# Turning back riding outputs by a DMA transposition, and placing one PSUM eviction behind another copy, in a two-layer memory transformer on one core

## The chip, the core and the metric

The kernel runs on one core of one Trainium2 chip. The metric is the device time of one execution in microseconds (us). The kernel before took 1631.83 us, the median of three runs (1628.36, 1632.63 and 1631.83). A further execution was profiled; all views below are of that one.

The engines go by the profile's names: PE (matmuls) with PEld (its weight loads), DVE (vector), ACT (scalar), POOL (GpSimd) and SP, which here issues nearly all the DMAs. L497 is line 497 of the kernel before.

## The reference, cut to what matters

Two layers of attention with a carried memory, each followed by a dense ReLU block; both layers use the same weights. x is 2048 tokens by 512, in 64 segments of 32 tokens. There are 32 heads of 128; the memory is 8 tokens.

```python
for s in range(n_seg):                       # strictly in order: mem is carried
    h = concat([mem, xs])                    # 8 + 32 tokens
    q, k, v = h @ Wq, h @ Wk, h @ Wv         # 512 -> 32 x 128
    p = softmax(where(mask, q @ k.T * scale, -1e9))
    o = (p @ v) @ Wo                         # 32 x 128 -> 512
    mem = o[:, :8]; outs.append(o[:, 8:])

x = x + A(layernorm(x)); x = x + B(layernorm(x))   # layer 0
x = x + A(layernorm(x)); x = x + B(layernorm(x))   # layer 1
# B: relu(x @ w1) @ w2, 512 -> 1376 -> 512
```

## The kernel before, in words

**Steps.** The recurrence over segments is the spine. Step k (k = 0 to 67) works on segment k of layer 0 and, four segments behind, on segment k-4 of layer 1, side by side. The order of PE, DVE, ACT and SP is written out by hand (`manual_schedule`): each of them executes its instructions in the order of the code of `step`. POOL's order is the scheduler's.

**One step on PE.** First the q and k products of heads 0 to 15 (`qk`, L601, three batches, evicted at L605 and L607); then the products of the memory tokens with Wv (`memory_values`, L348); in even steps also the values of layer 1 (`values1`); then scores (L641). Then the q and k products of heads 16 to 31, the transposition of the first half's probabilities (`transpose_p`, L680, copied out by DVE and ACT at L681), the second scores, and P times V of the first half (`weighted_v`, L695). Next come fillers, which have their operands ready and cover the softmax of the second half: values for later steps (`v1`, `v0`), dense products (L530, L548), output products (L468, L471). Then the second half's `transpose_p`, more fillers, its P times V, the output product of the memory tokens (`output_mem`, L648), its copy wm_sb (L959), and four small matmuls that turn it (mt, L981). Its copies HT (L984, DVE) and HTm (L986, ACT) open the next step.

**Values go through DRAM.** `group_values` (L341 to L354) makes a [128, 512] product with four column tiles, copies it from PSUM to the tile VmS on ACT (L353), and stores it to DRAM from SP (L354); `load` (L383) brings it back into Vs in the layout that L695 wants. VmS has three buffers. In a step that makes both `v1` and `v0`, four VmS follow one another, so the fourth waits until the first has been stored. The products of `v1` and the second of `v0` take their PSUM tiles from the pool `fill`, which has two buffers and also serves the dense products and the last P times V tile (L688).

**Riders.** The tile HTm holds the memory tokens of a step in 16 columns; the other 16 columns of the 32-wide matmul would be empty. They carry 16 tokens of a layer 0 segment, whose values so come for nothing. In the same way OTm, the operand of `output_mem`, carries 16 tokens of layer 1 outputs of every other block of 64 tokens. Such outputs leave mt with the model dimension on the partitions. ACT copies them into rT (L991), 16 columns in each of four steps. When a block's four pieces are there, in every fourth step (k = 8, 12, ... 64), `riders_back` (L489) turns them back with four matmuls by the identity into a PSUM tile rp of the pool `fill` (L497; L499 for the block of the last time, k = 64), and `riders_add` (L502, L506) adds rp on DVE to the block's residual R. Both stand behind the first q and k products of the step, ahead of `memory_values`.

**Token pairs.** The tile xe (one buffer) holds 128 tokens of x, loaded by `load_pair` in steps with k % 4 = 1, and read last by `pair_normalize` on DVE (L248) at the first q and k batch of a step with k % 4 = 0. Its normalised copy is transposed by a DMA from SP (`transpose_dma`, L264), as are the dense blocks.

Of the kernel before, what the change touches and what calls it, by code (L numbers as in the profile page):

```python
# [7 lines left out]
BF = mybir.dt.bfloat16  # L8
F32 = mybir.dt.float32
# [13 lines left out]
def kernel(  # L23
# [14 lines left out]
    nc = tc.nc  # L38
# [8 lines left out]
    NC4 = Dm // 128  # L47
# [9 lines left out]
    const = ctx.enter_context(tc.tile_pool(name="const", bufs=1))  # L57
    wk = ctx.enter_context(tc.tile_pool(name="wk", bufs=2))
    dram = ctx.enter_context(tc.tile_pool(name="vdram", bufs=2, space=DRAM))
    ps_c = ctx.enter_context(tc.tile_pool(name="ps_c", bufs=3, space=PSUM))  # L60
    ps_s = ctx.enter_context(tc.tile_pool(name="ps_s", bufs=1, space=PSUM))
    ps_wo = ctx.enter_context(tc.tile_pool(name="ps_wo", bufs=1, space=PSUM))
    ps_fill = ctx.enter_context(tc.tile_pool(name="ps_fill", bufs=2, space=PSUM))
# [8 lines left out]
    def rides(b):  # L72

        return b % 2 == 0 and 0 <= b <= RIDE_LAST

    def place(b):

        if rides(b):
            return b + 4, 0 if b == RIDE_LAST else 64
        return b + 2, 64  # L80
# [97 lines left out]
    ident = const.tile([128, 128], BF)  # L178
# [20 lines left out]
    mhalf_t = const.tile([128, 1], F32)  # L199
    nc.vector.memset(mhalf_t[:], -0.5)  # L200

    HTs, HTms = [], []
    for i in range(2):
        t = const.tile([128, NC4, 2, L], BF, name=f"HT{i}")
        nc.vector.memset(t[:], 0.0)
        HTs.append(t)
        t = const.tile([128, NC4, 32], BF, name=f"HTm{i}")
        nc.vector.memset(t[:], 0.0)
        HTms.append(t)
    Vs = const.tile([128, H * Dh], BF)  # L210
    PL = 64 + L
    Pf = const.tile([128, 7 * PL + 128], BF)
# [4 lines left out]
    OTx1 = const.tile([128, H // 2, 128], BF)  # L217
    OTm = const.tile([128, H, 32], BF)
    nc.gpsimd.memset(OTm[:], 0.0)
    rT = const.tile([128, 1 + NC4, 64], BF)  # L220
    nc.gpsimd.memset(rT[:, 0, :], 0.0)
    hT = const.tile([128, NFC, 128], BF)
    nc.gpsimd.memset(hT[F_LAST:128, NFC - 1, :], 0.0)

# [1 line left out]
    for a in range(2):  # L226
        t = ps_s.tile([128, 512], F32, name=f"sp{a}")
# [5 lines left out]
    vmds, vds = {}, {}  # L233
# [45 lines left out]
    def tokens_T(s, lo, n):  # L279

        c = SEG * (s % 4) + lo
        return pairs["T", s // 4][:, :, c:c + n]

    spare = {}
# [51 lines left out]

    vps = {}

    def group_values(lhsT, ii, dst, pool, tag, q, lo=0, hi=NC4, spare=False):  # L341
        if lo == 0:
            vps[tag] = pool.tile([128, 512], F32, tag=tag, name="vp")
        vp = vps[tag]
        for c4 in range(lo, hi):
            for j in range(4):
                n = 4 * ii + j
                nc.tensor.matmul(vp[32 * j:32 * j + 32, :], lhsT=lhsT(c4), rhs=Wv_sb[:, c4, n * 512:(n + 1) * 512],  # L348
                                 start=(c4 == 0), stop=(c4 == NC4 - 1), tile_position=(0, 32 * j))
        if hi < NC4:  # L350
            return
        VmS = wk.tile([128, 512], BF, tag="dnT" if spare else "VmS", bufs=1 if spare else 3, name="VmS")
        nc.scalar.copy(out=VmS[:], in_=vp[:])  # L353
        q.dma_start(out=dst[ii].rearrange("j t e -> (j t) e"), in_=VmS[:])  # L354

    def dram_values(name, tag, bufs):
        return dram.tile([2, 4, 32, 512], BF, tag=tag, bufs=bufs, name=name)
# [2 lines left out]

        return s >= 4 and s % 2 == 0

    def values0(s, ii, q=None, lo=0, hi=NC4):

        if ii == 0 and lo == 0:
            vds[0, s] = dram_values("vd0", "vd0", 4)
        t = tokens_T(s, 0, SEG)
        group_values(lambda c4: t[:, c4, :], ii, vds[0, s], *((ps_fill, "fill") if ii else (ps_c, "c")), q or nc.sync, lo, hi)

    def values1(k, ii, spare=False):  # L370

# [115 lines left out]
    rps = {}  # L487

    def riders_back(b):  # L489

        i, r = place(b)
        rp = rps[b] = ps_fill.tile([128, Dm], F32, tag="fill", name="rp")
        flat = rT[:].rearrange("p c t -> p (c t)")
        for c4 in range(NC4):
            cols = slice(c4 * 128, (c4 + 1) * 128)
            if r:
                nc.tensor.matmul(rp[:, cols], lhsT=flat[:, 64 * c4:64 * c4 + 128], rhs=ident[:], start=True, stop=True)  # L497
            else:
                nc.tensor.matmul(rp[0:64, cols], lhsT=rT[:, 1 + c4, :], rhs=ident[:], start=True, stop=True,  # L499
                                 tile_position=(0, 0))  # L500

    def riders_add(b):  # L502

        (i, r), rp = place(b), rps[b]
        R = R_tiles[i]
        nc.vector.tensor_tensor(out=R[r:r + 64, :], in0=R[r:r + 64, :], in1=rp[r:r + 64, :], op=ALU.add)  # L506
# [167 lines left out]
    def transpose_p():  # L674

        for p, copy in ((0, nc.vector.tensor_copy), (1, nc.scalar.copy)):
            tp = ps_c.tile([128, 4, 2, L], F32, tag="c")
            for sl in range(4):
                c = PL * (4 * p + sl)
                nc.tensor.matmul(tp[:, sl], lhsT=Pf[:, c:c + 128], rhs=ident_q, start=True, stop=True)  # L680
            copy(out=PT[:, 4 * p:4 * p + 4], in_=tp[:])  # L681
# [38 lines left out]
    def outputs_x(k, hf, pvs, q, copy, layers=(0, 1)):  # L720
        for a in layers:
            if (q, a) in pvs:
                h0, n = 16 * hf + 8 * q, L - ahead(k, a)
                c = 64 * a + SEG * (k % 2)
                ot = OTx1 if hf else OTx0[:, k // 2 % 2]
                copy(out=ot[:, 8 * q:8 * q + 8, c:c + n], in_=pvs[q, a][:, :, L - n:L])  # L726
# [7 lines left out]
    def step(k):  # L734
        act = [a for a in range(2) if 0 <= k - a * DELTA < NSEG]
        even = k % 2 == 0
        p = k // 2
# [10 lines left out]
        ride = ride_of(k)  # L748
        back = k // 2 - 4 if k % 4 == 0 and rides(k // 2 - 4) else None
        lone = k == NSTEP - 1  # L750
        HT, HTn = HTs[k % 2], HTs[(k + 1) % 2]
        HTm, HTmn = HTms[k % 2], HTms[(k + 1) % 2]
# [50 lines left out]
        qks = qk(HT, 0, act, after0)  # L803
        if back is not None:
            riders_back(back)
            riders_add(back)
        if dt is not None and not lone and not ahead_T:
            dense_normalize(dt)
        q = nc.sync
# [33 lines left out]
        if not even:  # L843
            i = p + 2 if p % 2 else p + 4
# [22 lines left out]

        def v0(ii):
            if fills_v0(k):
                values0(k + 3, ii)  # L870

        def v1(ii):
            if even and k >= DELTA:
# [26 lines left out]
            outputs_m(k, 0, pvs, 1)  # L900
            outputs_x(k, 0, pvs, 1, nc.scalar.copy)
        v0(0)
        v0(1)
        if k == 2:
            set_products(3, 5)
        hs = (0, 0, 1, 2, 3) if fills_v0(k) else (0, 2, 3, 3, 3)
# [9 lines left out]
        with tc.high_priority(offset=PRIO):  # L916
            for a in act:
                probabilities(1, ess, a, k)
            if first:
                hand_on(dw)  # L920
            transpose_p()
            if k == 0:
                set_evict(3, 0)
                set_products(3, 1)
            if k == 1:
                set_evict(3, 4)
            if k == 2:
                set_evict(3, 5)
                set_products(3, 6)
            if first:  # L930
                block_moments(dw)
# [6 lines left out]
        with tc.high_priority(offset=PRIO):  # L938
            pvs = weighted_v(1, act)
            for q2 in range(2):  # L940
                outputs_m(k, 1, pvs, q2)
            head = act[:1] if nx is not None and nw % 2 == 0 else act
            outputs_x(k, 1, pvs, 0, nc.vector.tensor_copy, head)
            if first:
                block_normalize(dw)
            outputs_x(k, 1, pvs, 1, nc.vector.tensor_copy, head)
            for q2 in range(2):
                outputs_x(k, 1, pvs, q2, nc.vector.tensor_copy, [a for a in act if a not in head])
            if dw is not None and dw >= 3 and not final:
                store(dw)  # L950
            if k == 2:
                set_evict(3, 6)
            if cont:
                output_mem(wo, 0, H - hh)
                if k == 0:
                    set_evict(3, 1)
                    set_values(3, 2, 4)
                output_mem(wo, H - hh, H)
                nc.scalar.copy(out=wm_sb[:], in_=wo[:])  # L959
            if k == 2:  # L960
                set_products(3, 7)
# [12 lines left out]
        s = rider(k + 1)  # L974
        if s is not None:
            nc.gpsimd.tensor_copy(out=HTmn[:, :, 2 * M:32], in_=tokens_T(s, 16 * ((k + 1) % 2), 16))
        if cont:
            with tc.high_priority(offset=PRIO):
                mt = ps_c.tile([128, NC4, 32], F32, tag="c", name="mt")
                for c4 in range(NC4):  # L980
                    nc.tensor.matmul(mt[:, c4, :], lhsT=wm_sb[:, c4 * 128:(c4 + 1) * 128], rhs=sel[:],  # L981
                                     start=True, stop=True)
                lo, hi = cont[0], cont[-1] + 1
                nc.vector.tensor_copy(out=HTn[:, :, lo:hi, 0:M],  # L984
                                      in_=mt[:, :, lo * M:hi * M].rearrange("p c (a m) -> p c a m", m=M))
                nc.scalar.copy(out=HTmn[:, :, lo * M:hi * M], in_=mt[:, :, lo * M:hi * M])  # L986
                if k == 2:
                    set_evict(3, 7)
                if ride is not None:
                    c = 32 * ride[1] + 16 * ride[2]  # L990
                    nc.scalar.copy(out=rT[:, 1:1 + NC4, c:c + 16], in_=mt[:, :, 16:32])  # L991
        if sooner is not None:
            dense_h(sooner, *hs[3:5])
        if w is not None:
# [7 lines left out]
    with tc.manual_schedule(engines={mybir.EngineType.PE, mybir.EngineType.DVE, mybir.EngineType.SP,  # L1002
# [30 lines left out]
        i = NT - 1  # L1033
# [47 lines left out]
```

## Time and profile before

| what | value |
|---|---|
| median of three runs | 1631.83 us |
| the profiled execution: its own time, its span | 1629.76 us, 1628.1 us |
| PE, DVE, ACT, POOL busy | 98%, 66%, 53%, 17% |
| granted PE clock | 1.00 |
| mean DMA rate | 76 GB/s |
| matmuls of `riders_back` (L497, L499) | 56 and 4 |
| `riders_add` (L506) | 15, 692 ns each |
| VmS evictions (L353) | 298, 587 ns each |
| DMA transpositions (L264) | 42 |

The span is the time from the first to the last instruction. PE's busy time is the length of the stretches in which a matmul is under way; matmuls are pipelined, so the duration of one (about 0.2 us for 128 columns) is not what it adds: what it adds is the distance from its start to the next one's start. In the timeline view several instructions of one line are merged into one row, which gives the start of the first, the time to the end of the last, and in brackets how long the engine had stood idle before, and for what.

The steps can be read from the starts of the first L601 group of each: step 12 runs from 300.22 to 323.79 us, step 13 to 348.85, step 14 to 372.69. In the middle of the kernel four steps together take about 94.4 us.

### The profile page before, as it was taken

To read this page: it belongs to the slowest core of one execution; us is meant where nothing else is said; L and a number is where in the kernel's file an instruction comes from. 1 tells how busy PE (TensorE), PEld (TensorE's weight loads), DVE (VectorE), ACT (ScalarE), POOL (GpSimd) and SP (SyncE) were. 2 spreads that over 40 slices of the span, in tenths; PEclk is the share of its full clock that TensorE was granted. 3 is DMA by queue.
4 is the path that set the end of the run, shared out by engine and by line. 5 is a ranking of instruction groups with operands and counts; after the bars stand their busy time and mean duration, and the time that the engine had idled before them with its cause. 6 is when DMAs were issued, how large, how long until landed. Compare 5 with 4: busy or idle time off the path is not lost. (4 is left out here: it accounts for less than half of the span.)

```text
span 1628.1 us, 83294 instructions
## 1 busy us (share of the span) xinstructions
PE 1587.8 (98%) x37231; PEld 1179.9 (72%) x37316; DVE 1079.7 (66%) x2592; ACT 858.3 (53%) x2424; POOL 269.1 (17%) x517
## 2 busy tenths in 40 slices
PE   7899999999999999999999999999999999999998
PEld 4677777777777777777777777777777777777766
DVE  4556766776676677667667766666776666667654
ACT  3455555555555555555555555555555555555543
POOL 1102111111111112111111111111111111111100
PEclk9999999999999999999999999999999999999999
DMA  9832222222222222222222221222222122221111
GB/s 346 258 93 61 72 68 66 69 57 69 56 65 76 71 65 63 64 55 66 74 74 61 66 66 50 71 69 76 60 70 62 56 64 76 66 69 47 54 46 30
DMA packets 132245, 124.14 MB, mean 76 GB/s; under 512 B 36392, under 2 KB 121808, under 8 KB 131152
## 3 DMA queue, kind: packets, MB, share of 16 engines
q1 hardware_dynamic: 129328, 114.62, 24.1%
q8 instruction: 292, 4.78, 1.3%
q0 software_dynamic: 2560, 4.20, 1.2%
q14 instruction: 65, 0.53, 0.1%
HBM read 65.81 MB, written 45.35 MB: 68 GB/s over the span
## 5 line engine op out<-in xcount | busy, mean ns | idle before, releaser
L601 PE MATMUL qp<-HT,Wq_sb 128*128 128x80 bf16 (+1 forms) x8704 | 368.7, 199 | 1.7 <-issue 0.7
L601 PE MATMUL qp<-HT,Wk_sb 128*128 128x80 bf16 (+1 forms) x8704 | 367.7, 199 | 0.6 <-ACT QT L605 0.3
L601 PEld LDWEIGHTS <-Wq_sb 128*128 128x128 bf16 x8704 | 328.3, 99 | 20.3 <-issue 11.9
L601 PEld LDWEIGHTS <-Wk_sb 128*128 128x128 bf16 x8704 | 329.7, 99 | 2.8 <-issue 0.4
L607 DVE CAST KT<-qp 128x480 bf16<-128x480 f32 (+3 forms) x340 | 199.4, 586 | 178.5 <-PE qp L601 172.5
L605 ACT CAST QT<-qp 128x480 bf16<-128x480 f32 (+3 forms) x340 | 172.0, 506 | 207.7 <-PE qp L601 205.3
L353 ACT CAST VmS<-vp 128x512 bf16<-128x512 f32 x298 | 172.0, 587 | 129.2 <-PE vp L348 122.9
L671 POOL TENSOR_TENSOR Pf<-es,sm 128x320 bf16<-128x320 f32 x187 | 135.0, 722 | 590.8 <-ACT QT L605 181.5
L656 DVE TENSOR_REDUCE mx<-sp 128x8 f32<-128x320 f32 x256 | 114.5, 486 | 110.2 <-PE sp L641 109.8
L661 ACT ACTIVATE es<-es 128x320 f32<-128x320 f32 x256 | 110.9, 469 | 77.5 <-DVE es L659 71.2
L668 DVE TENSOR_REDUCE sm<-es 128x8 f32<-128x320 f32 x256 | 120.5, 471 | 24.0 <-ACT es L661 13.6
L348 PE MATMUL vp<-Wv_sb,HTm 128*32 128x512 bf16 x2144 | 128.2, 380 | 2.0 <-issue 1.4
L648 PE MATMUL sp<-Wo_sb,OTm 128*32 128x512 bf16 x2144 | 128.2, 380 | 0.3 <-DMA Wo_sb<-in_A_Wo_dram 0.3
L348 PE MATMUL vp<-Wv_sb,HT 128*32 128x512 bf16 x2048 | 122.6, 380 | 0.0
L468 PE MATMUL wox<-Wo_sb,OTx 128*128 128x512 bf16 x434 | 112.4, 379 | 7.3 <-issue 4.8
L659 DVE TENSOR_TENSOR es<-sp,mx 128x320 f32<-128x320 f32 x256 | 113.3, 481 | 1.1
L726 DVE CAST OTx<-pv 128x256 bf16<-128x256 f32 (+1 forms) x256 | 85.7, 385 | 39.1 <-ACT OTm L718 39.0
L243 POOL TENSOR_TENSOR rstd<-rstd,mhalf_t 128x1 f32<-128x1 f32 x85 | 46.9, 552 | 391.0 <-DVE rstd L242 390.9
L718 ACT CAST OTm<-pv 128x64 bf16<-128x64 f32 (+1 forms) x512 | 93.4, 253 | 31.2 <-PE pv L695 31.2
L681 ACT CAST PT<-tp 128x320 bf16<-128x320 f32 x136 | 58.3, 429 | 67.5 <-PE tp L680 67.2
L726 ACT CAST OTx<-pv 128x256 bf16<-128x256 f32 (+1 forms) x256 | 78.7, 363 | 28.0 <-PE pv L695 28.0
L681 DVE CAST PT<-tp 128x320 bf16<-128x320 f32 x136 | 66.8, 491 | 39.5 <-PE tp L680 38.5
(122 smaller groups left out, 1928.1 us busy)
## 6 DMA issues: line engine op xcount, KB each, us to landing
vd<-VmS SPq DMA_DIRECT2D x164, 128.0 KB
Vs<-vd SPq DMA_DIRECT2D x164, 128.0 KB
vmd<-VmS SPq DMA_DIRECT2D x134, 128.0 KB
Vs<-vmd SPq DMA_DIRECT2D x254, 32.0 KB
Vs<-vmd SPq DMA_DIRECT2D x120, 64.0 KB
Wv_sb<-in_A_Wv_dram SPq DMA_DIRECT2D x4, 1024.0 KB
Wq_sb<-in_A_Wq_dram SPq DMA_DIRECT2D x4, 1024.0 KB
Wk_sb<-in_A_Wk_dram SPq DMA_DIRECT2D x4, 1024.0 KB
```

Of the source, the lines that this page charges most:

```text
L348: nc.tensor.matmul(vp[32 * j:32 * j + 32, :], lhsT=lhsT(c4), rhs=Wv_sb[:, c4, n * 512:(n + 1) * 512], start=(c4 == 0), stop=(c4 == NC4 - 1 ...
L353: nc.scalar.copy(out=VmS[:], in_=vp[:])
L601: nc.tensor.matmul(qp[:, hi, 0:ncol], lhsT=W_sb[:, c4, h * Dh:(h + 1) * Dh], rhs=HT[:, c4, a_lo:a_hi, :], start=(c4 == 0), stop=(c4 == NC4 ...
L605: nc.scalar.copy(out=dst[:, 0:nh, a_lo * L:a_hi * L], in_=qp[:, 0:nh, 0:ncol])
L607: nc.vector.tensor_copy(out=dst[:, 0:nh, a_lo * L:a_hi * L], in_=qp[:, 0:nh, 0:ncol])
L648: nc.tensor.matmul(wo[32 * j:32 * j + 32, :], lhsT=OTm[:, h, :], rhs=Wo_sb[:, h, :], start=(h < 4), stop=(h >= H - 4), tile_position=(0, 3 ...
L656: nc.vector.tensor_reduce(out=mxs[a][:], in_=sp_tiles[a], axis=AX.X, op=ALU.max)
L659: nc.vector.tensor_tensor(out=es[:], in0=sp_tiles[a], in1=mxs[a][:].unsqueeze(2).to_broadcast([128, 8, L]), op=ALU.subtract)
L668: nc.vector.tensor_reduce(out=sm[:], in_=es[:], axis=AX.X, op=ALU.add)
L671: eng.tensor_tensor(out=P[:, :, 64 * a:64 * a + L], in0=es[:], in1=sm[:].unsqueeze(2).to_broadcast([128, 8, L]), op=ALU.mult)
L681: copy(out=PT[:, 4 * p:4 * p + 4], in_=tp[:])
L726: copy(out=ot[:, 8 * q:8 * q + 8, c:c + n], in_=pvs[q, a][:, :, L - n:L])
```

## The change

Three things change.

1. The two HTm tiles become views of one tile rT [128, 4, 128]: columns 0 to 31 and 32 to 63 are the two HTm, columns 64 to 127 the riding outputs (which stood in a tile of their own). All of rT is zeroed at the start by DVE.
2. `riders_back` no longer uses PE, but for the block at k = 64: SP issues one DMA transposition of the whole of rT into a tile rb, which takes the buffer of xe. `riders_add` moves from its place ahead of `memory_values` to the end of the step's output copies (behind the L726 copies of the second half), and reads rb in SBUF and not rp in PSUM.
3. The second eviction of layer 0's values, with its store, is held back where s = k + 3 is above 5: it stands behind `transpose_p` of the second half, so that ACT copies the transposed probabilities (L681) first. In steps 6, 10, ... 50 and 52, 54, ... 60 this applies (17 steps). The unused argument for cutting the value products into ranges is dropped.

```diff
-        HTms.append(t)
+        HTms.append(rT[:, :, 32 * i:32 * i + 32])
...
-    def group_values(lhsT, ii, dst, pool, tag, q, lo=0, hi=NC4, spare=False):
+    def group_values(lhsT, ii, dst, pool, tag, q, spare=False, later=False):
...
+        def evict():
+            VmS = wk.tile([128, 512], BF, tag="dnT" if spare else "VmS", bufs=1 if spare else 3, name="VmS")
+            nc.scalar.copy(out=VmS[:], in_=vp[:])
+            q.dma_start(out=dst[ii].rearrange("j t e -> (j t) e"), in_=VmS[:])
+        if later:
+            return evict
+        evict()
...
     def riders_back(b):
         i, r = place(b)
+        if r:
+            t = wk.tile([128, NC4, 128], BF, tag="xe", bufs=1, name="rb")
+            nc.sync.dma_start_transpose(out=t[:], in_=rT[:].rearrange("p c t -> p (c t)"))
+            rps[b] = t[:].rearrange("p c d -> p (c d)")
+            return
...
-            if r:
-                nc.tensor.matmul(rp[:, cols], lhsT=flat[:, 64 * c4:64 * c4 + 128], rhs=ident[:], start=True, stop=True)
...
         if back is not None:
             riders_back(back)
-            riders_add(back)
+            if place(back)[1] == 0:
+                riders_add(back)
...
-        v0(1)
+        evict_v0 = v0(1)
...
             transpose_p()
+            if evict_v0 is not None:
+                evict_v0()
...
                 outputs_x(k, 1, pvs, q2, nc.vector.tensor_copy, [a for a in act if a not in head])
+            if back is not None and place(back)[1]:
+                riders_add(back)
...
-                    c = 32 * ride[1] + 16 * ride[2]
-                    nc.scalar.copy(out=rT[:, 1:1 + NC4, c:c + 16], in_=mt[:, :, 16:32])
+                    c = 64 + 32 * ride[1] + 16 * ride[2]
+                    nc.scalar.copy(out=rT[:, :, c:c + 16], in_=mt[:, :, 16:32])
```

More of the change, by code (lines that the diff above doesn't have):

```diff
@@ L200 @@
     nc.vector.memset(mhalf_t[:], -0.5)
+    rT = const.tile([128, NC4, 128], BF)
+    nc.vector.memset(rT[:], 0.0)
     HTs, HTms = [], []
@@ L206 @@
         HTs.append(t)
-        t = const.tile([128, NC4, 32], BF, name=f"HTm{i}")
-        nc.vector.memset(t[:], 0.0)
-        HTms.append(t)
+        HTms.append(rT[:, :, 32 * i:32 * i + 32])
     Vs = const.tile([128, H * Dh], BF)
@@ L219 @@
     nc.gpsimd.memset(OTm[:], 0.0)
-    rT = const.tile([128, 1 + NC4, 64], BF)
-    nc.gpsimd.memset(rT[:, 0, :], 0.0)
     hT = const.tile([128, NFC, 128], BF)
@@ L335, in set_store @@
             q.dma_start(out=set_dram[j][:, 512 * lo:512 * hi], in_=src)
-    vps = {}
-    def group_values(lhsT, ii, dst, pool, tag, q, lo=0, hi=NC4, spare=False):
[L342 to L345, printed above, removed]
+    def group_values(lhsT, ii, dst, pool, tag, q, spare=False, later=False):
+        vp = pool.tile([128, 512], F32, tag=tag, name="vp")
+        for c4 in range(NC4):
             for j in range(4):
@@ L349, in group_values @@
                                  start=(c4 == 0), stop=(c4 == NC4 - 1), tile_position=(0, 32 * j))
[L350 to L354, printed above, removed]
+        def evict():
[5 more added lines that the diff above has]
+        evict()
     def dram_values(name, tag, bufs):
@@ L361, in first_rider, with values0 @@
         return s >= 4 and s % 2 == 0
-    def values0(s, ii, q=None, lo=0, hi=NC4):
-        if ii == 0 and lo == 0:
+    def values0(s, ii):
+        if ii == 0:
             vds[0, s] = dram_values("vd0", "vd0", 4)
         t = tokens_T(s, 0, SEG)
-        group_values(lambda c4: t[:, c4, :], ii, vds[0, s], *((ps_fill, "fill") if ii else (ps_c, "c")), q or nc.sync, lo, hi)
+        return group_values(lambda c4: t[:, c4, :], ii, vds[0, s], *((ps_fill, "fill") if ii else (ps_c, "c")), nc.sync,
+                            later=ii == 1 and s > 5)
     def values1(k, ii, spare=False):
@@ L491, in riders_back @@
         i, r = place(b)
+        if r:
[3 more added lines that the diff above has]
+            return
         rp = rps[b] = ps_fill.tile([128, Dm], F32, tag="fill", name="rp")
-        flat = rT[:].rearrange("p c t -> p (c t)")
         for c4 in range(NC4):
-            cols = slice(c4 * 128, (c4 + 1) * 128)
-            if r:
[L497 to L500, printed above, removed]
+            nc.tensor.matmul(rp[0:64, c4 * 128:(c4 + 1) * 128], lhsT=rT[:, c4, 64:128], rhs=ident[:], start=True,
+                             stop=True, tile_position=(0, 0))
     def riders_add(b):
@@ L869, in v0 @@
             if fills_v0(k):
-                values0(k + 3, ii)
+                return values0(k + 3, ii)
         def v1(ii):
```

## The prediction

> **What bounds the kernel.** I read the page first: how busy the engines are, and the clock.
>
> ```profile
> PE 1587.8 (98%) x37231; PEld 1179.9 (72%) x37316; DVE 1079.7 (66%) x2592; ACT 858.3 (53%) x2424; POOL 269.1 (17%) x517
> PEclk9999999999999999999999999999999999999999
> ```
>
> PE is busy for 98% of the span, at full clock: only 40 us in all are without a matmul. So the time is the sum of what PE issues, and a change gains what it takes off PE, or from those 40 us. Who causes them is in the view of waits: on PE itself, most entries are fixed gaps of 0.2 to 0.4 us; one entry bears on the change, PE pv L695 waiting for ACT PT L681, 2.0 us in two waits.
>
> **Part 1, the four matmuls that go.** PE's timeline around `riders_back`, in step 12 (with it) and in step 13 (without):
>
> ```profile
> 304.23 0.74 PE L601 MATMUL qp<-HT,Wk_sb 128*128 128x80 bf16 x16
> 304.81 0.39 PE L497 MATMUL rp<-ident,rT 128*128 128x128 bf16 x4
> 305.12 1.91 PE L348 MATMUL vp<-Wv_sb,HTm 128*32 128x512 bf16 x32
> ```
> ```profile
> 327.80 0.74 PE L601 MATMUL qp<-HT,Wk_sb 128*128 128x80 bf16 x16
> 328.47 0.83 PE L348 MATMUL vp<-Wv_sb,HTm 128*32 128x512 bf16 x12
> ```
>
> One L601 matmul lasts 0.20 us (199 ns, page part 5), so the last of the sixteen starts at 304.23 + 0.74 - 0.20 = 304.77, and L348 follows 0.35 us later. In step 13 the same distance is 328.47 - 328.34 = 0.13 us. So the four matmuls add 0.22 us to PE's order, not the 4 x 0.22 us of their durations. Over the 14 steps (k = 8 to 60): **14 x 0.22 = 3.1 us**. The last block (L499) stays on PE.
>
> Does PE use the 0.22 us? All that PE does next in the step hangs on PE itself: the next wait, for scores (308.69), has its K copy done at 305.50 and its mask at 305.90, and everything behind shifts along. The PSUM buffer that rp no longer takes is asked for by `values1` at 306.86, when its former users, of the step before, are long done. So I count all of it.
>
> **What part 1 adds.** One DMA transposition on SP, each of the 14 times; at step 12 it stands between these two rows:
>
> ```profile
> 300.21 1.94 SPq L383 DMA_DIRECT2D Vs<-vmd  x4
> 306.83 1.20 SPq L354 DMA_DIRECT2D vmd<-VmS  x2
> ```
>
> It waits for rT's last piece (L991, 300.35) and for rb's buffer, which `pair_normalize` reads until 303.12. The same operation on an equal tile (L264) holds SP for 1.2 us: 303.1 to 304.4. Behind it on SP stands the vmd store, which has nothing to store until 306.83. So SP has 2.4 us to spare. The transfer itself is shown at step 13, where such a transposition precedes the store directly:
>
> ```profile
> 328.61 1.20 SPq L264 DMA_TRANSPOSE dnT<-xn  x1
> 330.18 1.69 SPq L354 DMA_DIRECT2D vmd<-VmS  x2
> 332.83 1.33 SPq L383 DMA_DIRECT2D Vs<-vmd  x4
> ```
>
> From the end of the store's issue (331.87) to the load that waits for it: 0.96 us, and 309.84 - 308.03 = 1.81 us in step 12 with no transposition ahead. So a transposition just ahead does not make the store land later. I take 0; the upper bound is in the rivals. The reader of rb, `riders_add`, comes 18 us later.
>
> `riders_add` itself (0.69 us) leaves DVE ahead of the first maximum, where DVE idled 2.48 us (no gain), and goes here:
>
> ```profile
> 320.65 1.15 DVE L726 CAST OTx<-pv 128x256 bf16<-128x256 f32 x4 [0.90 <-ACT OTm L718]
> 323.52 0.22 DVE L984 CAST HT<-mt 128x64 bf16<-128x64 f32 x1 [1.72 <-PE mt L981]
> ```
>
> Behind it is HT, which opens the next step and is on the path; but DVE stood idle 1.72 us for it. 0.69 us fits and leaves 1.0 us. With both operands in SBUF it has no row here; even at twice the time, 1.4 us, it fits: 0. Without that cover it would cost 14 x 0.69 = 10 us. rb holds xe's buffer until 322.5; the next load into xe is issued at 334.20. The shared tile rT makes POOL's and ACT's writes of HTm wait for the transposition, by then 10 us old. The one larger memset at the start (128 x 256 in the changed kernel's list of instructions) stands for three small ones: 0.
>
> [...]
>
> **Part 2, the eviction held back.** Where it matters is step 54, whose ACT rows read:
>
> ```profile
> 1313.84 0.65 ACT L353 CAST VmS<-vp 128x512 bf16<-128x512 f32 x1
> 1316.46 0.58 ACT L353 CAST VmS<-vp 128x512 bf16<-128x512 f32 x1 [1.97 <-DMA vd<-VmS]
> 1316.94 0.43 ACT L681 CAST PT<-tp 128x320 bf16<-128x320 f32 x1
> ...
> 1317.42 0.37 PE L695 MATMUL pv<-PT,Vs 40*128 40x40 bf16 x16 [1.69 <-ACT PT L681]
> ```
>
> The fourth VmS waits for a buffer, that is for a store; the copy PT stands behind it, and PE waits 1.69 us for PT. Held back, PT would be done about 1315.0 (its transposition ran at 1314.08), and this wait goes. What is late next? The second half of L695 writes a tile of the two-buffer pool `fill`, whose turn is the buffer of the very product that the late eviction reads (v1, v1, v0, one dense product, then L695). In the changed kernel's order this shows as a new wait for ACT on that matmul. PE now waits for the eviction's end, 1317.04 instead of PT's end, 1317.37: only **0.33 us** of the 1.69 come back. Step 38 has the same picture (eviction 0.61 us late, PE 0.34 us): 0.3 us. In the common step (step 14), PT today ends just in time; afterwards PT ends some 0.5 us earlier and the eviction where PT ended (367.85 + 0.43 + 0.58 - 0.11 overlap = 368.75, against 368.82): 0, and within 0.1 us either way, that is -0.9 to +0.9 us over the 9 steps of this kind. In six further steps (6, 18, 26, 52, 56, 60) the second half of L695 starts 0.05 to 0.1 us behind the end of the first: 0.3 us together. Where no dense product follows (52, 56, 60) the held-back copy ends some 0.9 us later, at the start of the output copies (L718), whose reader on PE is 0.8 us further on: 0. Sum: **0.33 + 0.3 + 0.3 = about 1.0 us**.
>
> **Sum.** 1629.76 - 3.1 - 1.0 = 1625.7 us against the profiled execution. The median of the runs is 2.1 us above that execution; shifted by the same 4.1 us it gives 1627.7. Both ends are likely; I forecast **1627.0 us**, which is 0.3% below the median. A difference of 0.3% (4.9 us) is about what a measurement of this kernel can tell from none, and the forecast lies on that line.
>
> **Rivals.**
> - *The wait does go.* If the new wait on the `fill` buffer does not bind, the whole of the PT waits comes back: 1.7 + 0.3 and up to 0.9 in small ones. 1629.76 - 3.1 - 2.9 = 1623.8. Against it: the order's new wait. For it: stores are late by chance, and other executions may have more late ones.
> - *The 0.22 us are absorbed.* If a wait later in the step with a fixed time (a DMA's round trip) ends last, part 1 gives nothing: 1629.76 - 1.0 = 1628.8, or 1630.8 from the median. For it: the Vs loads have only some 0.7 us to spare in step 12 (last issue done 312.36; by the store's 1.81 us it lands at 314.2; L695 starts at 314.89). Against it: these loads hang on PE's own products and so shift along.
> - *Slower: the transposition holds up the vmd round trip.* If it ended late enough to delay the vmd store, the Vs loads would land later by as much, and PE would wait for what exceeds 0.7 us. The slowest transposition in the trace (xnT, issued 312.40) still moves a few packets at 316.2, 3.9 us after its issue, where 1.2 to 2.1 us is usual. A store held back by 2 us costs (2 - 0.7) x 14 = 18 us: 1629.76 - 4.1 + 18 = 1644. It decides from an end later than 306.83 + 0.7 = 307.5; the usual end is 305.2, the slowest 307.0. Step 13 speaks against it. [...]
>
> That the change does not do what it says is excluded by its order: PE's differs by just those 56 matmuls, SP's by 14 transpositions.
>
> **Numbers.** The forecast 0.68, the wait goes 0.12, absorbed 0.12, slower 0.08. The forecast's half below the 0.3% line and all of the first rival are "faster": 0.33 + 0.12 = 0.45. The other half and the absorbed case are "same": 0.35 + 0.12 = 0.47. Slower: 0.08. The range takes in the first rival, less the common step's 0.9 us and as much again for what late stores add or spare by chance (1622.0), and the absorbed case from the median with 0.9 us above (1631.7). The slower rival is left out.
>
> **What would show it.** Part 1: no L497, L348 0.13 us behind the last L601 in steps 8, 12, ... 60, those steps 0.22 us shorter (23.57 to 23.35), a transposition on SP at about 3 us into them, DVE still idle ahead of HT. Part 2: PT ahead of the fourth VmS, and PE's waits at L695 named for ACT VmS and not PT, about 0.3 us shorter. I am wrong if PE waits for a DMA at L695, if HT starts later, or if steps other than these change.

## The result and the profile after

The changed kernel takes **1624.24 us**, the median of six runs (1623.53 to 1625.36); the kernel before, beside it, 1630.6 us (six runs, 1628.36 to 1632.63, the three of above among them). The ratio is 0.9958, with a 95% interval of 0.9948 to 0.9968: faster by 0.42%. The forecast was 1627.0, so the gain is larger than forecast. The profiled execution has a time of 1624.61 us and a span of 1622.9 us, 5.15 us less than that of before (1629.76 and 1628.1).

The page of the kernel after, the busy times of the engines:

```profile
PE 1584.0 (98%) x37175; PEld 1176.4 (72%) x37260; DVE 1078.7 (66%) x2591; ACT 859.2 (53%) x2424; POOL 269.9 (17%) x516
```

PE has 56 matmuls fewer and is busy 3.8 us less; its share is the same. Where the 5.15 us come from is read step by step, from the distances between the starts of the first L601 groups: steps 8, 12, ... 60 (those that turn riders back) give -3.8 us, steps 10, 14, ... 58 give -1.1, the first six steps and the two ends -0.3, all others together +0.1. The -0.3 says nothing about the change: in the 14 traces of this document the first six steps take 128.9 to 132.4 us together, with no order by kernel.

**The riders' steps.** An undisturbed one takes 23.22 us where it took 23.57. That is 0.35 us, not the forecast 0.22. PE's timeline of the kernel after at the place of `riders_back`, in step 20 (start, duration, engine, line):

```profile
492.64 0.74 PE L601 MATMUL qp<-HT,Wk_sb 128*128 128x80 bf16 x16
493.31 1.05 PE L343 MATMUL vp<-Wv_sb,rT 128*32 128x512 bf16 x16
```

The last L601 matmul starts at 492.64 + 0.74 - 0.20 = 493.18; the product of the memory tokens (L343, formerly L348) follows 0.13 us later, as in a step without riders. So 0.22 us came off here, as forecast. The other 0.13 us come off later in the step. First DVE, then PE, in step 20 of the kernel before:

```profile
497.93 0.89 DVE L656 TENSOR_REDUCE mx<-sp 128x8 f32<-128x320 f32 x2 [2.48 <-PE sp L641]
498.85 0.89 DVE L659 TENSOR_TENSOR es<-sp,mx 128x320 f32<-128x320 f32 x2
```
```profile
499.75 1.03 PE L601 MATMUL qp<-HT,Wq_sb 128*128 128x80 bf16 x24
500.81 1.02 PE L601 MATMUL qp<-HT,Wk_sb 128*128 128x80 bf16 x24
```

and in the kernel after:

```profile
497.29 0.89 DVE L656 TENSOR_REDUCE mx<-sp 128x8 f32<-128x320 f32 x2 [2.98 <-PE sp L641]
498.09 0.88 DVE L659 TENSOR_TENSOR es<-sp,mx 128x320 f32<-128x320 f32 x2
```
```profile
499.11 1.03 PE L601 MATMUL qp<-HT,Wq_sb 128*128 128x80 bf16 x24
500.03 1.02 PE L601 MATMUL qp<-HT,Wk_sb 128*128 128x80 bf16 x24
```

From the first maximum (L656) to the first subtraction (L659) it was 0.92 us and is 0.80: before, L659 started 0.03 us behind the end of the second maximum; now it starts 0.08 us ahead of that end, as it did and does in all steps without riders. This holds in all 14 riders' steps. A step without riders in the kernel before, step 11:

```profile
285.25 0.89 DVE L656 TENSOR_REDUCE mx<-sp 128x8 f32<-128x320 f32 x2 [1.26 <-PE sp L641]
286.06 0.88 DVE L659 TENSOR_TENSOR es<-sp,mx 128x320 f32<-128x320 f32 x2
```

The exponentials and the QT copies on ACT follow as much earlier, and a QT copy frees the PSUM buffer of the next K batch: from the Wq group to the Wk group PE took 1.06 us and takes 0.92. So `riders_add`, which stood ahead of the maxima, had been costing 0.13 us a step, though DVE idled 2.48 us behind it. Why, is the subject of experiments 2 to 4.

**What part 1 added.** SP in step 20 of the kernel after:

```profile
491.63 1.24 SPq L494 DMA_TRANSPOSE rb<-rT  x1
495.02 1.20 SPq L349 DMA_DIRECT2D vmd<-VmS  x2
```

The transposition stands 3.0 us into the step and holds SP until 492.87; the vmd store comes 2.15 us later, when its data are there. DVE at the end of the step:

```profile
508.70 1.15 DVE L726 CAST OTx<-pv 128x256 bf16<-128x256 f32 x4 [0.90 <-ACT OTm L718]
509.88 0.69 DVE L506 TENSOR_TENSOR R<-R,rb 64x512 f32<-64x512 f32 x1
511.56 0.23 DVE L989 CAST HT<-mt 128x64 bf16<-128x64 f32 x1 [0.99 <-PE mt L986]
```

`riders_add` takes 0.69 us also with both operands in SBUF and leaves DVE idle for 0.99 us ahead of HT (forecast 1.0). One thing the prediction had otherwise: the transposition is not 10 us old when POOL writes the shared tile rT. In all 14 cases POOL's next copy into rT (L981) waits for it, until 5.4 to 7.4 us into the step (step 60: 3.6). Nothing on the path follows from this: PE's one wait for a POOL copy into this tile, 0.6 us, was there before (0.7 us, HTm).

**Part 2.** PE's longest waits at L695 are named for the eviction and no longer for ACT's copy PT. From the views of waits before and after (us in total, times, longest):

```profile
PE pv L695 <- ACT PT L681: 2.0, 2, 1.7
```
```profile
PE pv L695 <- ACT VmS L348: 1.0, 2, 0.7
```

A late store now shows like this, ACT and then PE in step 50:

```profile
1215.28 0.43 ACT L681 CAST PT<-tp 128x320 bf16<-128x320 f32 x1
1216.46 0.59 ACT L348 CAST VmS<-vp 128x512 bf16<-128x512 f32 x1 [0.75 <-DMA vd<-VmS]
```
```profile
1216.02 0.39 PE L695 MATMUL pv<-PT,Vs 40*128 40x40 bf16 x17
1217.10 0.35 PE L695 MATMUL pv<-PT,Vs 40*128 40x40 bf16 x15 [0.69 <-ACT VmS L348]
```

PT is done in time and the first half of L695 runs; the second half waits for the eviction, whose PSUM buffer it takes. The steps that run longer are 26, 38 and 54 before (0.2, 0.5 and 1.85 us longer than their like) and 18, 30 and 50 after (0.5, 0.2 and 0.85). Undisturbed steps of this kind take 23.86 us in both.

The steps are not drawn afresh in each execution. In the six traces of kernels that turn the riders back on PE, step 38 is over 0.1 us longer in all six and step 54 in five; in the eight traces of kernels with the transposition, neither is in any, but 18 and 50 are in seven each. So the -1.1 us of the profiled pair is not part 2 alone, but also a shift of the steps that have late stores.

What holding back is worth in one late step can be read from the start of the late eviction. At its old place, a step in which it waits for a store is longer than 23.86 us by as much as it starts later than 19.08 us into the step (step 54 before: 20.93, 1.85 us longer; step 38: 19.57, 0.50). Held back, the same holds from 19.42 us on (step 50 after: 20.28, 0.86; step 26 of `evict_only`: 21.13, 1.71). Each fits to 0.01 us, and so do all such steps of the twelve traces without a buffer of its own for this eviction. So a late store still costs, but 0.34 us less.

### The profile page after: what moved, and what is told of

It is laid out like the page before. It is cut to its first block, busy times and chain, and to the rows that moved or that the text cites. A ratio compares the mean times of both kernels' runs of the same rounds, so it can differ in the third digit from the quotient of the medians.

```text
span 1622.9 us, 83239 instructions
## 1 busy us (share of the span) xinstructions
PE 1584.0 (98%) x37175; PEld 1176.4 (72%) x37260; DVE 1078.7 (66%) x2591; ACT 859.2 (53%) x2424; POOL 269.9 (17%) x516
## 5 line engine op out<-in xcount | busy, mean ns | idle before, releaser
L601 PE MATMUL qp<-HT,Wq_sb 128*128 128x80 bf16 (+1 forms) x8704 | 368.7, 199 | 1.5 <-DVE HT L989 0.6
L601 PE MATMUL qp<-HT,Wk_sb 128*128 128x80 bf16 (+1 forms) x8704 | 367.7, 199 | 0.0
L601 PEld LDWEIGHTS <-Wq_sb 128*128 128x128 bf16 x8704 | 328.3, 99 | 20.1 <-issue 11.6
L601 PEld LDWEIGHTS <-Wk_sb 128*128 128x128 bf16 x8704 | 329.7, 99 | 0.8
L348 ACT CAST VmS<-vp 128x512 bf16<-128x512 f32 x298 | 172.4, 588 | 121.5 <-PE vp L343 118.5
L656 DVE TENSOR_REDUCE mx<-sp 128x8 f32<-128x320 f32 x256 | 114.5, 486 | 117.0 <-PE sp L641 116.6
L343 PE MATMUL vp<-Wv_sb,rT 128*32 128x512 bf16 x2144 | 128.2, 380 | 1.9 <-issue 1.3
L343 PE MATMUL vp<-Wv_sb,HT 128*32 128x512 bf16 x2048 | 122.7, 380 | 0.3 <-issue 0.3
L659 DVE TENSOR_TENSOR es<-sp,mx 128x320 f32<-128x320 f32 x256 | 113.1, 480 | 0.5
L726 DVE CAST OTx<-pv 128x256 bf16<-128x256 f32 (+1 forms) x256 | 85.7, 385 | 38.9 <-ACT OTm L718 38.8
L681 ACT CAST PT<-tp 128x320 bf16<-128x320 f32 x136 | 58.3, 429 | 72.4 <-PE tp L680 70.4
L681 DVE CAST PT<-tp 128x320 bf16<-128x320 f32 x136 | 66.8, 492 | 40.2 <-PE tp L680 39.1
L726 ACT CAST OTx<-pv 128x256 bf16<-128x256 f32 (+1 forms) x256 | 78.7, 362 | 28.1 <-PE pv L695 28.1
```

The source lines that it names most:

```text
L601: nc.tensor.matmul(qp[:, hi, 0:ncol], lhsT=W_sb[:, c4, h * Dh:(h + 1) * Dh], rhs=HT[:, c4, a_lo:a_hi, :], start=(c4 == 0), stop=(c4 == NC4 ...
L656: nc.vector.tensor_reduce(out=mxs[a][:], in_=sp_tiles[a], axis=AX.X, op=ALU.max)
L659: nc.vector.tensor_tensor(out=es[:], in0=sp_tiles[a], in1=mxs[a][:].unsqueeze(2).to_broadcast([128, 8, L]), op=ALU.subtract)
```

## The experiments

**1. Each part alone.** `evict_only` is the kernel before with the held-back eviction alone; `dma_only` is the kernel after with the eviction in its old place.

```diff
# evict_only, against before
-        v0(1)
+        evict_v0 = v0(1)
...
             transpose_p()
+            if evict_v0 is not None:
+                evict_v0()
# dma_only, against after
-                            later=ii == 1 and s > 5)
+                            later=False)
```

> The kernel before with the third part of the change alone (the second eviction of layer 0's values held back behind the copy of the transposed probabilities). My account: PE's wait moves from that copy to the late eviction itself, through the two-buffer PSUM pool, so only about 0.3 us of each late store comes back: 0.5 to 1.5 us less than before in all (ratio 0.9991 to 0.9997), and the four PE matmuls of the riders and their steps unchanged at 23.57 us. Rival (the wait goes altogether): about 3 us less (0.998). If late stores vary from run to run, the spread of the runs shrinks little in my account.

> The changed kernel without the held-back eviction: only the DMA transposition with the addition at the end of the step. The trace of the changed kernel shows clean rider steps 0.35 us shorter, 0.22 us of it at the four matmuls and 0.13 us at a K product of the second half. So I expect 14 x 0.35 = 4.9 us less than before (ratio 0.9970), 23.21 us for a clean rider step. Rival (the DMA transposition also costs something through late loads or stores): 3 us less or fewer, with rider steps that wait for a DMA.

Beside runs of the kernel before with a median of 1631.68 us, `evict_only` took 1630.29 us (ratio 0.9986, interval 0.9975 to 0.9998) and `dma_only` 1625.56 us (0.9963, 0.9953 to 0.9973). So the transposition brings nearly all of the gain, and the eviction about 1.4 us by the medians. The interval of `evict_only` takes in both my 0.9991 to 0.9997 and, at its edge of 0.9975, the rival's 0.998, so the times alone do not decide between them. The views of waits show what becomes of the wait at `weighted_v`, in `evict_only` (whose lines stand 7 further down) and in `dma_only`:

```profile
PE pv L702 <- ACT VmS L355: 2.0, 3, 1.5
```
```profile
PE pv L695 <- ACT PT L681: 1.9, 2, 1.0
```

With the eviction held back PE waits for the eviction; without it, for PT. The wait changes its name and stays, as the new wait on the `fill` buffer has it, and not as the rival has it.

**2. The add's place.** `dma_early_add` is the kernel after with `riders_add` where it stood before; `pe_add_before_mask` is the kernel before with riders_back and riders_add one place earlier, ahead of the last mask copy (L631) instead of behind it.

```diff
# dma_early_add, against after
             riders_back(back)
-            if place(back)[1] == 0:
-                riders_add(back)
+            riders_add(back)
# pe_add_before_mask, against before
+            if n == 2 and back is not None:
+                riders_back(back)
+                riders_add(back)
             if n > 0:
                 masks(act[n - 1:n], 0)
...
-        if back is not None:
-            riders_back(back)
-            riders_add(back)
```

> The changed kernel with the addition of the riders put back to its old place on DVE, directly ahead of the first maxima, reading the result of the DMA transposition. Theory: the 0.13 us that rider steps gained beyond the four matmuls come from the addition's leaving that place (with it, the first difference es starts 0.03 us behind the second maximum's end; without it, 0.08 us ahead of that end). Then rider steps take 23.34 us here, and the whole is 14 x 0.13 = 1.8 us slower than the changed kernel. Rival: they come from PE's matmuls or the PSUM buffer that went: then 23.21 us, the same as the changed kernel. Second rival: the addition waits there for the transposition and delays the maxima: over 23.4 us.

> The kernel before with the riders turned back on PE as before, but the addition on DVE one place earlier, ahead of the last mask copy rather than behind it, so that it no longer stands directly ahead of the maxima. If standing directly ahead of the maxima is what costs 0.13 us, rider steps take 23.57 - 0.13 = 23.44 us and the whole is 1.8 us faster than before (0.9989). If the addition costs it wherever it stands in that stretch (or if PE's matmuls do), 23.57 us and the same time as before.

Undisturbed riders' steps: 23.35 us in the first (23.22 after), 23.45 in the second (23.57 before). By the medians, 1626.17 us (ratio 0.9964, 0.9952 to 0.9976) and 1629.3 us (0.9985, 0.9975 to 0.9995); the intervals are wider than the 1.8 us in question, so the steps decide. The 0.13 us belong to the add's place and to nothing else in the change, and one place earlier (with the four matmuls, which moved along) is enough. DVE in step 20 of `pe_add_before_mask`:

```profile
494.58 0.69 DVE L506 TENSOR_TENSOR R<-R,rp 64x512 f32<-64x512 f32 x1
495.31 0.49 DVE L631 CAST sp<-maskb 128x320 f32<-128x320 bf16 x1
498.16 0.89 DVE L656 TENSOR_REDUCE mx<-sp 128x8 f32<-128x320 f32 x2 [2.36 <-PE sp L641]
498.97 0.88 DVE L659 TENSOR_TENSOR es<-sp,mx 128x320 f32<-128x320 f32 x2
```

The maxima still wait over 2 us for PE, and L659 follows 0.81 us behind the first. So it is not the time that the add takes. My theory now was that the add delays L659 when it stands directly ahead of the maxima.

**3. Next to the maxima, an instruction more, or the add's size?** Three kernels, one execution of each, read by their steps: the kernel before with a memset of 128x1 behind the add; the kernel after with that memset at the add's old place; the kernel before with the add cut to 8 of its 512 columns.

```diff
# add_then_memset, against before
             riders_add(back)
+            nc.vector.memset(small[:], 0.0)
# memset_alone, against after
             if place(back)[1] == 0:
                 riders_add(back)
+            nc.vector.memset(small[:], 0.0)
# add_narrow, against before
-out=R[r:r + 64, :], in0=R[r:r + 64, :], in1=rp[r:r + 64, :]
+out=R[r:r + 64, 0:8], in0=R[r:r + 64, 0:8], in1=rp[r:r + 64, 0:8]
```

> The kernel before, with a memset of 128x1 on DVE directly behind riders_add, so that the add no longer stands next to the maxima. Theory (the add must stand directly ahead of the maxima to delay the subtraction L659): L659 starts 0.08 us before the second maximum ends, as in steps without riders; rider steps 23.567 - 0.13 = 23.44 us. Rival (any extra instruction between the mask copies and the maxima delays it, or the add's place ahead of the wait matters however far): 0.03 us behind the maximum's end, 23.57 us.

> The kernel after, with a memset of 128x1 on DVE at the old place of riders_add (behind the first q and k products, ahead of the maxima). Theory (it is the add that delays, not one instruction more): rider steps stay at 23.22 us, L659 starts 0.08 us before the second maximum's end. Rival (any instruction there delays): 23.35 us, 0.03 us behind it.

> The kernel before, with riders_add cut to the first 8 of 512 columns (the rest of the riding outputs is not added). If the delay comes from the add's kind (two operands, 64 partitions) it stays: L659 0.03 us behind the second maximum's end, rider steps 23.57 us. If it comes from the add's length (0.69 us, which would fall to about 0.1 us), it goes: 0.08 us before the end, 23.44 us. I expect the first, 0.6 to 0.4, since the add has ended over 2 us before the first maximum starts.

In `add_then_memset` L659 still starts 0.03 us behind the second maximum's end, and the step takes 23.57 us: the theory of adjacency falls. In `memset_alone` nothing is delayed (0.08 us ahead of the end, 23.22 us): an instruction more is not it. In `add_narrow` the delay is whole (0.03 behind, 23.57 us) although the add takes 0.17 us. DVE of `add_then_memset`, step 20:

```profile
495.05 0.69 DVE L507 TENSOR_TENSOR R<-R,rp 64x512 f32<-64x512 f32 x1
495.81 0.06 DVE L808 MEMSET small<- 128x1 f32 x1
498.23 0.89 DVE L657 TENSOR_REDUCE mx<-sp 128x8 f32<-128x320 f32 x2 [2.36 <-PE sp L642]
499.14 0.89 DVE L660 TENSOR_TENSOR es<-sp,mx 128x320 f32<-128x320 f32 x2
```

0.91 us between the starts, with a memset between. So a mask copy ends the effect of the add, a memset does not, and the add's length plays no part. The mask copy reads SBUF (maskb), the memset reads nothing, and the maxima read only PSUM.

In every riders' step the add works on partitions 64 to 127; L659 reads mx from partition 0 on, and between the two nothing else reads SBUF. My theory now was that this is the condition: L659 is held until the second maximum has ended when its own SBUF input starts at partition 0 and the last read of DVE from SBUF started at partition 64.

**4. The theory put to the test.** One kernel, `quadrants`: the kernel before with different things in different steps, one execution. What (a) to (d) expect is what the theory gives.

```diff
-            riders_add(back)
+            riders_add(back, 0 if k % 12 == 0 and k < 64 else None)
+            if k % 12 == 8:
+                nc.vector.tensor_copy(out=small[:, 1:2], in_=small[:, 0:1])
+        if k % 4 == 3 and 8 < k < 60:
+            nc.vector.tensor_copy(out=small[64:128, 1:2], in_=small[64:128, 0:1])
```

> The kernel before with four things tried in different steps of one execution. [...] (a) Steps 16, 28, 40, unchanged: L659 starts 0.03 us behind the second maximum's end, 23.57 us a step. (b) Steps 8, 20, 32, 44, 56, a copy of 128x1 from SBUF to SBUF, partitions 0 to 127, behind the add: 0.08 us before that end, 23.44 us where 23.57 stood. (c) Steps 12, 24, 36, 48, 60, the add on partitions 0 to 63 (the riding outputs then go to other rows of the residual): 0.08 us before, 23.44. (d) Steps 11, 15, ... 59, which have no add, with a copy of 64x1 from SBUF to SBUF on partitions 64 to 127 ahead of the maxima: 0.03 us behind, where these steps had 0.08 before; the step 21.90 to 22.03 us. Rival (an add of two operands delays, wherever it stands in the partitions, until a mask copy follows): (b) 0.08 before or 0.03 behind, (c) 0.03 behind and 23.57, (d) 0.08 before and 21.90.

All four came out as the theory has it, in every step of their kind:

| steps | ahead of the maxima | L659 against the second maximum's end | undisturbed step |
|---|---|---|---|
| 16, 28, 40, 52 | the add at partition 64 | 0.03 us behind | 23.57 us |
| 8, 20, 32, 44, 56 | the add, then a 128x1 copy from partition 0 | 0.08 us ahead | 23.45 us |
| 12, 24, 36, 48, 60 | the add at partition 0 | 0.08 us ahead | 23.45 us |
| 11, 15, ... 59 | a 64x1 copy at partition 64, no add | 0.03 us behind | 22.02 us (21.90 before) |

The last row is the strongest: a copy of 64 numbers makes a step 0.12 us longer. DVE in step 11 of this kernel:

```profile
283.39 0.15 DVE L813 COPY small<-small 64x1 f32<-64x1 f32 x1
284.62 0.89 DVE L659 TENSOR_REDUCE mx<-sp 128x8 f32<-128x320 f32 x2 [1.08 <-PE sp L644]
285.53 0.89 DVE L662 TENSOR_TENSOR es<-sp,mx 128x320 f32<-128x320 f32 x2
```

and in step 20, where a copy from partition 0 follows the add:

```profile
494.81 0.69 DVE L509 TENSOR_TENSOR R<-R,rp 64x512 f32<-64x512 f32 x1
495.53 0.15 DVE L811 COPY small<-small 128x1 f32<-128x1 f32 x1
497.98 0.89 DVE L659 TENSOR_REDUCE mx<-sp 128x8 f32<-128x320 f32 x2 [2.30 <-PE sp L644]
498.79 0.88 DVE L662 TENSOR_TENSOR es<-sp,mx 128x320 f32<-128x320 f32 x2
```

0.91 us between the starts where the last SBUF read began at partition 64, 0.81 where it began at partition 0.

**5. The slower rival's price.** `dma_late` is the kernel after with the transposition moved on SP from ahead of the two vmd stores to right behind them.

```diff
-            riders_back(back)
             if place(back)[1] == 0:
+                riders_back(back)
                 riders_add(back)
...
                 memory_values(k)
+            if back is not None and place(back)[1]:
+                riders_back(back)
```

> The changed kernel with the DMA transposition moved on SP from ahead of the memory values' two stores to directly behind them, ahead of the stores of layer 1's values. This puts a price on the slower rival of the prediction. The transposition holds SP for 1.2 us there, so the later stores and the loads behind them are issued up to 1.2 us later. My estimate of what these loads have to spare is 0.7 us, so PE waits 0 to 0.5 us in the second half of the step: 0 to 7 us slower than the changed kernel in all, likeliest 3 us. If SP has more slack than I think, no change.

It took 1629.09 us (ratio to before 0.9982, 0.9973 to 0.9991), 5.4 us more than the kernel after beside it (1623.64, `after_again`). SP and PE in its step 20:

```profile
494.92 1.20 SPq L349 DMA_DIRECT2D vmd<-VmS  x2
496.21 1.24 SPq L494 DMA_TRANSPOSE rb<-rT  x1
497.54 1.00 SPq L349 DMA_DIRECT2D vd<-VmS  x2
...
502.25 0.31 SPq L383 DMA_DIRECT2D Vs<-vd  x1
```
```profile
503.43 0.56 PE L695 MATMUL pv<-PT,Vs 40*128 40x40 bf16 x31 [0.39 <-DMA Vs<-vd]
```

The transposition's 1.24 us of SP put off the stores of the layer 1 values and the loads behind them; the last load is issued 13.7 us into the step (13.0 in the kernel after), and PE waits 0.39 us for it. It comes 0.7 us later, so it had some 0.3 us to spare in this step. In the whole execution:

```profile
PE pv L695 <- DMA Vs<-vd: 3.9, 6, 0.8
```

In the kernel after this row does not occur. So a badly placed transposition does make PE wait for loads, though not by holding up the vmd store as the slower rival has it: the vmd stores stand ahead of it here and start when they did. The change put the transposition into the gap where SP waits for data. The price is not the same in each step: five of the 14 riders' steps (8, 16, 24, 28, 60) lose nothing, the others 0.15 to 0.86 us. In step 20 the first vd load is issued 2.5 us later than in the kernel after though its store is issued only 0.9 us later; how much of such late landings is the transposition's own traffic stays open.

**6. The buffer behind the late stores.** `after_again` is the kernel after once more; `after_xn` gives the held-back eviction a buffer of its own (that of xn); `dma_only_xn` gives the eviction that buffer in its old place.

```diff
# after_xn; dma_only_xn is the same without later=...
-                            later=ii == 1 and s > 5)
+                            later=ii == 1 and s > 5, spare="xn" if ii == 1 and s > 5 else None)
```

> The changed kernel once more, beside the kernels of this call on the same chip: 0.9958 of before as measured (0.995 to 0.997). In its profile late stores (the fourth VmS of a step waiting for the first one's store) should fall in other steps than in the first one, since they come by chance.

> The changed kernel with a buffer of its own for the held-back eviction (that of xn, which is free at that place), so that it no longer waits for the store of the step's first VmS. Theory: late stores cost the changed kernel what its profile shows at the second half of P times V (0.49 + 0.85 + 0.17 us) and nothing else, so 1 to 2 us less than the changed kernel (0.9990 of it), no wait of ACT VmS for a store in these steps, and less spread. Rival: a late store is late for everything, and the loads behind it on SP make PE wait elsewhere: the same time as the changed kernel.

> The same buffer, with the eviction not held back, so in its old place ahead of the copy of the transposed probabilities. If waiting for a buffer is the only reason why its place matters, this takes the same time as the version with both, within 0.05%: about 0.3 us more from the six steps in which the copy ends just too late. If its place itself matters (ACT's queue), it is slower than that version by over 1 us.

Beside runs of before with a median of 1631.55 us, the medians are 1623.64, 1623.84 and 1623.55 us, the ratios 0.9947 (0.9935 to 0.996), 0.9951 (0.9938 to 0.9965) and 0.995 (0.9937 to 0.9962): no difference that five runs of each, with intervals some 2 us to either side, can tell. My 1 to 2 us for the own buffer are not seen. In the profiled execution of `after_again` late stores cost only 0.4 us, so there was little left to save. They fell in steps 18 and 50, which were late in the first profile too: my expectation of other steps was wrong, and with it the idea that late stores come by chance alone. With the own buffer the eviction's place makes no difference either, within the same intervals; this agrees with the wait for a buffer being the only reason why its place matters, but does not show it. A fourth buffer for VmS was not run.

## Why the prediction was right, and where it was off

- **The four matmuls, 0.22 us a step: right to the hundredth.** The distance L601 to L343 is 0.13 us, and the 0.22 us arrive in the step's length (23.57 to 23.35 us in `dma_early_add`, which has this part without the moved add).
- **The step that failed: "`riders_add` itself (0.69 us) leaves DVE ahead of the first maximum, where DVE idled 2.48 us (no gain)".** It was worth 0.13 us a step, 14 x 0.13 = 1.8 us. DVE's idle time covered the 0.69 us of the add itself, not the 0.13 us that the add cost its successors. The evidence was in the trace: L659 stood 0.92 us behind the first maximum in riders' steps, 0.81 us (step 11: 286.06 - 285.25) in others. I compared PE's distances between steps with and without riders, but not DVE's. Part 1 is therefore 14 x 0.35 = 4.9 us; the trace gives 3.8, since seven riders' steps in this execution have stalls of PE of 0.07 to 0.56 us, 1.5 us together, against 0.4 us in three steps before. Their cause is open.
- **The transposition, 0: right by its place, as far as the traces tell.** The stalls just named leave room for a small price: over the 14 riders' steps they come to 0.3 to 0.8 us in the six traces without the transposition and to 0.5 to 1.6 us in the seven with it at its place. The ranges overlap, and no run separates it. Its end was estimated too early, too. I took 5.0 us into the step as usual and 6.8 as the slowest; in `dma_early_add`, where DVE is ready for rb at 5.7 us, it was there in time in six steps, in two DVE waited 0.1 us, and in six 0.4 to 1.7 us, until 7.35 us in the worst. The vmd store was issued at 6.39 us in all the same, and no wait of PE for a load is in the view. So an end near the point "later than 307.5" (7.3 us into the step) held nothing up; what costs in `dma_late`, 5.4 us, is the place on SP.
- **`riders_add` at its new place, 0: right.** 0.69 us as forecast, 0.99 us of cover left.
- **Part 2, about 1.0 us: right in kind.** PE's wait takes the eviction's name, undisturbed steps do not change, and a late store still costs. `evict_only` gives 1.4 us by the medians; the interval of its ratio, 0.02 to 0.25% of 1632 us or 0.3 to 4.1 us, takes in the 1.0. The size in a late step, 0.33 us in step 54, is borne out: 19.42 - 19.08 = 0.34 us. The third term, 0.3 us from six further steps, is so only in part: steps 6 and 60 take the same with the eviction held back alone (23.45 and 24.35 us) and without (23.44 and 24.34), and 52 and 56, 0.1 us shorter with it, are as short in `add_narrow` without it. Steps 18 and 26 had small late stores, 0.1 and 0.2 us, which holding back takes away. As an estimate from the trace before, 0.34 us each in 38 and 54 and these two make about 0.9 us.
- **The rivals.** That the wait goes is excluded by the new wait. That the 0.22 us are absorbed is excluded by the steps' lengths. That the transposition holds up the round trip did not happen; where the transposition stands badly on SP, in `dma_late`, the price is 5.4 us.

So the sum, with the one term put right, is 3.1 + 1.8 + 1.0 = 5.9 us, less what the stalls took; it was 5.15 us in the profiled execution, 6.4 by the medians. A further 1.2 us between forecast and result lie in the base: the median of before was 1631.83 in the three runs shown, 1630.6 in the six beside the result.

## What to carry to other kernels

Take a step that contains the instruction and a step that does not, and compare the distances on every engine, not only on the one that is the bound: what an instruction costs its successors (here 0.13 us a step) shows there, and its own duration and the idle time around it do not tell it. A DMA put into a hand-ordered queue puts off what stands behind it (the vd stores by 0.9 us in step 20 of `dma_late`), so it belongs where the queue waits for data anyway. A wait for one of several buffers need not go away when its instruction is moved behind another (PE waited 2.0 us for ACT PT in the kernel before, and 2.0 us for ACT VmS in `evict_only`): ask who takes the next buffer. And before calling a delay chance, see whether it comes again in the same steps of another execution.

## What the runs showed of the hardware

- On DVE, L659 starts 0.115 us later (0.03 us behind the end of the second maximum instead of 0.08 us before it) when the last read from SBUF began at partition 64 and its own SBUF input begins at partition 0. The maxima's reads from PSUM and a memset in between do not change this (`add_then_memset`: 0.03 us behind); a 0.15 us copy that reads SBUF from partition 0 takes the delay away (`quadrants`, step 20: 0.08 us ahead).
- A DMA transposition of 128x512 bf16 holds SP for 1.24 us in step 20 of the kernel after, 3.4 to 4.2 times the 0.37 and 0.29 us of a plain load (the medians of Vs<-vd and Vs<-vmd there), and in `dma_early_add` took up to 4.3 us from the start of its issue until DVE could read it (step 20: 3.01 to 7.35 us into the step); in eight of the 14 steps it was there within 2.85 us.
- Late stores go together with transfers of 16 KB of instructions. In the 14 traces, steps 10, 14, ... 58 number 182. Of the 51 that are over 0.1 us longer than 23.86 us, 46 have such a transfer starting 16.4 to 18.3 us into the step; of the other 131, 27 have one. One exception recurs: step 26 of the kernel before, 0.2 us longer without such a transfer there. This is a coincidence in traces, and no run changed the transfers to test it.
